# A gated recurrence and a highway layer on one core: two first units of 128 tokens, one shared set of work buffers and a new order

## The chip, the cores and the metric

The kernel runs on one core of a Trainium2 chip. The core has TensorE (PE) for matrix products and transposes, VectorE (DVE), ScalarE (ACT), GpSimd (POOL), and SyncE (SP), which here only starts transfers between the chip's main memory and the core's own memory. Every engine works through its own list of instructions in order and waits where a list says that another engine or a transfer must be done first. The metric is the time of one execution in microseconds (us); several runs are given by their median.

## The reference

```python
def _attn_ref(x, f_logit, lower_bound):              # x: (4, 6336, 256)
    sig = 1.0 / (1.0 + np.exp(-f_logit))
    f = lower_bound + (1.0 - lower_bound) * sig
    i = 1.0 - f
    for t in range(S):
        h = f[:, t] * h + i[:, t] * x[:, t]
        y[:, t] = h

def _moe_ref(x, w_h, w_t, b_t):                      # x: (25344, 256)
    H = np.maximum(x @ w_h, 0.0)
    T = 1.0 / (1.0 + np.exp(-(x @ w_t + b_t)))
    return T * H + (1.0 - T) * x
```

The second function takes the first one's output. Four sequences of 6336 tokens with 256 channels each go through a recurrence along the tokens, and then each token through a highway layer.

## The kernel before, in words

The 25344 tokens, all sequences in a row, are cut into units of 2, 4, 8 or twice 8 blocks of 128 tokens (list `parts`, 21 units numbered from 0). A unit's transfer puts consecutive tokens on each of 128 partitions. Each unit passes through these steps; the letter is the step's name in the order list, and the lines are those of the profile:

- `l` and `x` load f_logit and x (L261, on SP). `u` is the sigmoid of -f_logit (L273, on ACT).
- `i` transposes u on PE, so that channels lie on partitions (L297; two halves of 128 channels). `f` makes 1 - (1 - lower_bound) u from it (L312 on ACT, or L310 on DVE).
- `b` or `B` makes the product u times x (L288, on POOL, or on DVE where the list has a v), one half or the whole of a tile; `p` transposes it on PE, two tokens in one 32-bit word (L322).
- `s` is the recurrence, a scan on DVE from f and the transposed product (L331). Each scan goes on from the last column of the one before, so scans are strictly in order.
- `z` and `g` are the two matrix products of the highway layer on PE (L344, and L149 where the weights in place are used again). `t` is the sigmoid of z (L367, on ACT); `d` joins g and the scan's result on DVE (L374); `e` or `E` multiplies d by t (L388, on POOL, or on DVE with a v).
- `o` brings the result back to tokens on partitions and adds the two parts, with two matmuls for each 128 x 128 piece (L407, L408). `c` copies it out of the accumulators (L427 on ACT, L425 on DVE) and `w` stores it (L434, on SP).
- `k*n` are n dummy matmuls on zeros (L250, L149), which only keep PE busy; six more open the program (L168).

The numbers behind a letter are unit, part or chunk, and half; the number behind the colon is the buffer or the accumulator banks.

No scheduler decides anything: a long string, `order`, lists all steps, and each engine gets its own in the order of that string. SP's loads and stores share one queue in that order, so a store that waits for its copy also holds the loads behind it. Buffers are named in the string too. f_logit and x have five tiles each of 8 KB per partition; u has 4, the product 3, f 4, the scan 6, t 3, d 4 and the output 4 tiles of 4 KB, 28 in all, each kind its own; the last three units' output uses tiles of x. A step that writes a tile waits until the tile's former content has been read.

Parameters come first: `prm` holds lower_bound and b_t, is transposed on PE (`pc`, L212), and DVE makes three small constants of it (`cc`, L216 to L218), which f, d, the scaled weights (`WH`, `WT`) and the diagonal matrix `diag` (`dg`) need.

## Time and profile before

| | |
|---|---|
| Runs | 207.93, 206.80, 207.52 us, median 207.52 us |
| The profiled execution, first to last instruction | 205.8 us |
| Busy: PE, DVE, ACT, POOL | 194.8, 192.4, 190.7, 173.8 us |
| Moved by DMA | 78.67 MB, 382 GB/s over the span |
| Instructions on PE, DVE, ACT, POOL | 1850, 147, 182, 85 |

Busy time is the time in which an engine had an instruction at work, so overlaps count once. For PE it includes the dummy matmuls, and a busy PE is not PE at its peak. The span leaves out what lies before the first and behind the last instruction. In the rows of the profile, `128x1024 bf16<-128x1024 f16` are the shapes and types of result and operand, the first number behind a bar is the sum of busy time, the second the mean in nanoseconds of one instruction, and an arrow names what ended a wait. The clock that PE was granted reads 1.00 in nearly all stretches.

### The profile page before, as it was taken

The numbers are of one execution on the slowest core, as the hardware profiler recorded it, in microseconds if no ns is written. First come the engines' busy times: TensorE is split into PE (matmuls) and PEld (weight loads), VectorE is DVE, ScalarE is ACT, GpSimd is POOL, SyncE is SP. The second block draws the span as 40 slices with busy tenths as digits, with TensorE's granted clock in tenths as the row PEclk, the third lists the DMA queues.
The fourth block names the chain that finished last, engine by engine and source line by source line (L and its number), as shares of the span: only waits on it lengthen the run. The fifth ranks groups of instructions, "written<-read, shape, count | busy, mean of one in ns | idle before, by whom it ended". The sixth has DMA issues, their size and how long they took to land.

```text
span 205.8 us, 4646 instructions
## 1 busy us (share of the span) xinstructions
PE 194.8 (95%) x1850; PEld 135.7 (66%) x1850; DVE 192.4 (93%) x147; ACT 190.7 (93%) x182; POOL 173.8 (84%) x85
## 2 busy tenths in 40 slices
PE   7989999969989999999999999999999999999992
PEld 2555775746765747757757858657757868777671
DVE  0679999999999999999999999999999999999992
ACT  5197999999999999999999999999999999999992
POOL 3634696999999999979999869999899788999760
PEclk9999999999999999999999999999999999999999
DMA  6999999999999999999999999999999999853766
GB/s 191 375 427 419 417 420 419 414 413 426 416 426 427 414 422 410 432 408 427 426 408 426 427 412 425 419 422 427 414 411 407 334 411 382 344 212 140 277 225 234
DMA packets 16700, 78.67 MB, mean 382 GB/s; under 512 B 1828, under 2 KB 2344, under 8 KB 10792
## 3 DMA queue, kind: packets, MB, share of 16 engines
q1 hardware_dynamic: 16672, 78.39, 93.9%
q8 instruction: 14, 0.23, 0.4%
q14 instruction: 6, 0.05, 0.1%
q10 hardware_dynamic: 8, 0.00, 0.0%
HBM read 52.43 MB, written 25.95 MB: 381 GB/s over the span
## 4 chain that ended last, share of the span: by engine, by line
PE 56%; DVE 24%; ACT 7%; issue 5%; DMA 5%; SPq 0%; DVEq 0%; ACTq 0%
PE psum L344 17%; DVE y L331 15%; PE psum L149 13%; DVE d L374 7%; PE psum L407 7%; PE psum L408 7%; PE psum L322 6%; PE psum L297 5%; ACT f L312 4%; DMA x<-in_x_dram 4%; ACT t L367 2%; DMA l<-in_f_logit_dram 1%; ACT u L273 1%; PE psum L250 1%; ACT o L427 1%
## 5 line engine op out<-in xcount | busy, mean ns | idle before, releaser
L288 POOL TENSOR_TENSOR bv<-u,x 128x1024 bf16<-128x1024 f16 (+2 forms) x39 | 101.4, 2615 | 20.0 <-DVE d L388 10.9
L331 DVE TENSOR_TENSOR_SCAN y<-f,y,psum 128x1024 bf16<-128x1024 f16 (+6 forms) x40 | 103.7, 2612 | 0.5 <-PE psum L407 0.4
L344 PE MATMUL psum<-y,w_sb 128*128 128x512 bf16 (+1 forms) x240 | 79.6, 368 | 4.2 <-ACT f L312 1.9
L388 POOL TENSOR_TENSOR d<-d,t 128x1024 bf16<-128x1024 bf16 (+3 forms) x33 | 71.5, 2180 | 4.6 <-ACT o L427 1.3
L374 DVE SCALAR_TENSOR_TENSOR d<-y,ncc,psum 128x1024 bf16<-128x1024 bf16 (+2 forms) x60 | 62.7, 1084 | 1.1 <-PE psum L344 0.4
L149 PE MATMUL psum<-y,w_sb 128*128 128x512 bf16 x168 | 63.6, 379 | 0.0
L367 ACT ACTIVATE t<-psum,bt 128x1024 bf16<-128x1024 f32 (+2 forms) x60 | 57.4, 988 | 0.9 <-PE psum L344 0.5
L273 ACT ACTIVATE u<-l 128x2048 f16<-128x2048 f32 (+2 forms) x28 | 48.1, 1744 | 6.5 <-DMA l<-in_f_logit_dram 6.5
L312 ACT ACTIVATE f<-psum,ncc 128x1024 f16<-128x1024 f16 (+3 forms) x38 | 50.3, 1344 | 1.2 <-PE psum L297 1.2
L407 PE MATMUL psum<-diag,y 128*128 128x128 f16 x396 | 49.7, 219 | 0.2
L408 PE MATMUL psum<-ident_b,d 128*128 128x128 bf16 x396 | 49.7, 219 | 0.0
L408 PEld LDWEIGHTS <-d 128*128 128x128 bf16 x396 | 43.5, 112 | 3.8 <-DVE d L388 0.4
L427 ACT COPY o<-psum 128x1024 f32<-128x1024 f32 (+1 forms) x46 | 44.2, 997 | 1.6 <-ACT f L312 0.6
L407 PEld LDWEIGHTS <-y 128*128 128x128 bf16 x396 | 43.6, 112 | 2.7
L344 PEld LDWEIGHTS <-w_sb 128*128 128x128 f16 x240 | 23.0, 98 | 20.1 <-issue 0.8
L322 PE MATMUL psum<-ident_f,bv 128*128 128x128 f32 x198 | 29.4, 275 | 0.8 <-ACT f L312 0.7
L149 PEld LDWEIGHTS <-w_sb 128*128 128x128 f16 x168 | 16.4, 97 | 20.2 <-issue 5.9
L297 PE MATMUL psum<-ident_h,u 128*128 128x128 f16 x396 | 28.8, 221 | 0.8 <-DVE y L331 0.4
L297 PEld LDWEIGHTS <-u 128*128 128x128 f16 x396 | 25.1, 99 | 5.7 <-issue 1.2
L322 PEld LDWEIGHTS psum<-ident_f,bv 128*128 128x128 f32 x198 | 22.4, 141 | 5.8 <-ACT f L312 1.4
L388 DVE TENSOR_TENSOR d<-d,t 128x1024 bf16<-128x1024 bf16 (+3 forms) x20 | 11.3, 596 | 0.1
L149 PE MATMUL psum<-zeros 128*128 128x512 bf16 x39 | 10.6, 398 | 0.0
(34 smaller groups left out, 43.1 us busy)
## 6 DMA issues: line engine op xcount, KB each, us to landing
l<-in_f_logit_dram SPq DMA_DIRECT2D x23, 1024.0 KB, 13.6
x<-in_x_dram SPq DMA_DIRECT2D x23, 1024.0 KB, 14.2
out_dram<-o SPq DMA_DIRECT2D x43, 512.0 KB, 8.0
out_dram<-x SPq DMA_DIRECT2D x7, 256.0 KB, 2.0
out_dram<-o SPq DMA_DIRECT2D x6, 256.0 KB, 9.3
l<-in_f_logit_dram SPq DMA_DIRECT2D x2, 512.0 KB, 6.5
x<-in_x_dram SPq DMA_DIRECT2D x2, 512.0 KB, 7.3
l<-in_f_logit_dram SPq DMA_DIRECT2D x3, 256.0 KB, 2.8
```

The source lines that it names most:

```text
L149: return pe.add_instruction(mybir.InstMatmult(name=nc.get_next_instruction_name(), start_tensor_calc=start, stop_tensor_calc=stop, tile_si ...
L288: shared(pin(e.tensor_mul(st[n]["bv", s][:, a:c].rearrange("p k d j -> p k j d"), st[n]["u", s][:, 2 * a:2 * c].rearrange("p (k j) d -> p ...
L297: pin(nc.tensor.transpose(uT[:, j * P:(j + 1) * P], st[n]["u", s][:, j, h * P:(h + 1) * P], ident_h))
L312: pin(nc.scalar.activation(to, of, AF.Identity, scale=ncc[:, h:h + 1], bias=1.0))
L322: pin(nc.tensor.transpose(words[:, k:k + g * (P - 1) + 1:g], pair, ident_f))
L331: pin(nc.vector.tensor_tensor_scan(y[:, c:e], st[n]["f", h][:, c:e], data, 0.0 if fresh else carry[h], op0=ALU.mult, op1=ALU.add))
L344: pin(nc.tensor.matmul(p.part(a, e), w, data, start=ki == 0, stop=ki == NH - 1))
L367: pin(nc.scalar.activation(half(n, q, "t", m), z, AF.Sigmoid, bias=bt[:, m:m + 1]))
L374: pin(nc.vector.scalar_tensor_tensor(half(n, q, "d", m), y, ncc[:, m:m + 1], g, op0=ALU.mult, op1=ALU.max))
L388: shared(pin(e.tensor_mul(d, d, t)), not eng)
L407: pin(nc.tensor.matmul(o, st[n]["y", h][:, whole], diag[:, h], start=True, stop=False))
L408: pin(nc.tensor.matmul(o, half(n, q, "d", h)[:, cols], ident_b, start=False, stop=True))
```

## The change

There are 22 units in place of 21: the first two have one block of 128 tokens each, then come one of 2 and one of 4 blocks, and the rest as before with numbers one higher. A product of a unit with one block is made without interleaving two tokens, and transposed as it is.

lower_bound and b_t are loaded into tiles of their own and transposed apart (`pc` and `pb`); b_t is copied by ACT or DVE in a step of its own (`cb`).

All 4 KB tiles (u, product, f, scan, t, d, output) come from one set of 29 (28 before), and the ten 8 KB tiles serve f_logit and x alike. For units of up to 8 blocks f shares one tile for both halves, and so does the scan. The late units no longer take their output tiles from x.

In `products`, the line that picks the engine stands further up; the engine is still DVE where the list has a v, and POOL elsewhere.

The order list is new throughout. It has 23 dummy matmuls behind the first six, where there were 49. More products and gates are made in one piece: POOL has 20 products of a whole tile in place of 12, and 13 gates of 2048 columns in place of 5. DVE has 4 gates of 1024 and 4 of 2048 columns in place of 11 and 1.

Three places of the lists, word for word. Names left of an arrow are written, right of it read; `out_dram` is the output.

First, ACT at the start, before:

```order
L273 ACTIVATE u<-l 128x512 x2
L273 ACTIVATE u<-l 128x1024
L312 ACTIVATE f<-psum,ncc 128x256
L238 ACTIVATE w_sb<-w_raw,cc 128x256 x2
L312 ACTIVATE f<-psum,ncc 128x256
L367 ACTIVATE t<-psum,bt 128x256
L312 ACTIVATE f<-psum,ncc 128x512
L367 ACTIVATE t<-psum,bt 128x256
L273 ACTIVATE u<-l 128x2048
```

and with the change, from the first two sigmoids on:

```order
L289 ACTIVATE u<-l 128x256 x2
L343 ACTIVATE f<-psum,ncc 128x128 x2
L232 COPY bt<-psum 128x2
L289 ACTIVATE u<-l 128x512
L343 ACTIVATE f<-psum,ncc 128x128
L343 ACTIVATE f<-psum,ncc 128x256
L254 ACTIVATE w_sb<-w_raw,cc 128x256 x2
L289 ACTIVATE u<-l 128x1024
L254 ACTIVATE w_sb<-w_raw,cc 128x256 x2
L343 ACTIVATE f<-psum,ncc 128x512
L399 ACTIVATE t<-psum,bt 128x128
L399 ACTIVATE t<-psum,bt 128x256 x2
```

Three more 128-wide t follow, and then the first 2048-wide sigmoid. More and smaller instructions now stand ahead of it.

Second, ACT from the first 2048-wide sigmoid (unit 4) on, with the change:

```order
L289 ACTIVATE u<-l 128x2048
L343 ACTIVATE f<-psum,ncc 128x1024
L455 COPY o<-psum 128x256
L399 ACTIVATE t<-psum,bt 128x512 x2
L289 ACTIVATE u<-l 128x2048
L343 ACTIVATE f<-psum,ncc 128x1024 x2
L455 COPY o<-psum 128x512
L289 ACTIVATE u<-l 128x2048
L343 ACTIVATE f<-psum,ncc 128x1024
L399 ACTIVATE t<-psum,bt 128x1024 x2
L343 ACTIVATE f<-psum,ncc 128x1024
L289 ACTIVATE u<-l 128x2048
```

Here the sigmoids of units 4, 5, 6 and 7 come at closer intervals than those of units 3 to 6 before; behind the row printed last follow f, t, the sigmoid of the first part of unit 8, t, f, a copy of 256 columns, and the sigmoid of the second part.

Third, DVE up to its first 1024-wide scan, before:

```order
L331 SCALAR_TENSOR_TENSOR y<-f,y,psum 128x512 x2
L374 SCALAR_TENSOR_TENSOR d<-y,ncc,psum 128x256 x2
L374 SCALAR_TENSOR_TENSOR d<-y,ncc,psum 128x512
L288 TENSOR_TENSOR bv<-u,x 128x2x2x256
L388 TENSOR_TENSOR d<-d,t 128x256
L374 SCALAR_TENSOR_TENSOR d<-y,ncc,psum 128x512
L388 TENSOR_TENSOR d<-d,t 128x256
L388 TENSOR_TENSOR d<-d,t 128x512
L388 TENSOR_TENSOR d<-d,t 128x256
L331 SCALAR_TENSOR_TENSOR y<-f,y,psum 128x1024 x2
```

and with the change:

```order
L363 SCALAR_TENSOR_TENSOR y<-f,y,psum 128x512 x2
L309 TENSOR_TENSOR bv<-u,x 128x4x2x256
L406 SCALAR_TENSOR_TENSOR d<-y,ncc,psum 128x512 x2
L363 SCALAR_TENSOR_TENSOR y<-f,y,psum 128x1024 x2
L453 COPY o<-psum 128x1024
```

The gates of the first units have left DVE, and the whole product of unit 4 stands there in place of a half of unit 3's. The dummies between unit 3's and unit 5's transposes on PE are the steps `k*9:4`, `k*1:6` and `k*4:7` of the list; on SP, `l19.0:8` takes the 8 KB tile that `x15.0:8` had, and the product that frees it is `B15.0:19`.

The diff; of the order table its first two lines on each side stand for all:

```diff
@@ -39,9 +39,9 @@
     firsts = [b * S for b in range(B)]
 
 
-    CHUNK, GROUP = {17: 4, 18: 4}, {17: 2, 18: 2, 19: 2, 20: 1}
-    JOINED, FROM_X = (20,), (18, 19, 20)
-    parts = [(2,), (2,), (4,), (8,), (8,), (8,), (8,), (8, 8), (8, 8), (8, 8), (8, 8), (8, 8), (8, 8), (8, 8), (8,), (8,), (8,), (8,), (8,), (4,), (2,)]
+    CHUNK, GROUP = {18: 4, 19: 4}, {18: 2, 19: 2, 20: 2, 21: 1}
+    JOINED = (21,)
+    parts = [(1,), (1,), (2,), (4,), (8,), (8,), (8,), (8,), (8, 8), (8, 8), (8, 8), (8, 8), (8, 8), (8, 8), (8, 8), (8,), (8,), (8,), (8,), (8,), (4,), (2,)]
     units, at = [], 0
     for subs in parts:
         units.append((at, subs))
@@ -49,67 +49,67 @@
     assert at == B * S
 
     order = """
-k*4:0 l1.0:0 u1.0:0 i1.0.0:0 i1.0.1:1 l0.0:1 x0.0:0 x1.0:1 u0.0:1 b0.0.0:0 pc:2 wh i0.0.0:3 i0.0.1:4 WI k*1:5 cc
-p0.0.0:2 p0.0.1:5 k*16:6 l2.0:2 u2.0:2 wt b1.0.0:1 p1.0.1:6 f1.0:0 dgv f0.0v:1 f0.1v:2 s0.1:0 x2.0:2 WHv s0.0:1
...
+x0.0:0 l1.0:1 l0.0:2 u0.0:0 x1.0:3 pb:0 pc:1 cc u1.0:1 k*1:6 i0.0.1:7 f0.1:2 b0.0.0:3 i1.0.1:2 l2.0:4 f1.1:4 p0.0.1:3
+i0.0.0:4 f0.0v b1.0.0:5 p0.0.0:5 p1.0.1:6 i1.0.0:1 dg wh WI s0.1:6 cbv s0.0 p1.0.0:7 u2.0:7 i2.0.0:2 i2.0.1:0 s1.1:8
...
@@ -122,6 +122,12 @@
 
     def sb(shape, dtype, name, slot=0):
         return pool.tile(shape, dtype, tag=f"{name}{slot}", name=name)
+
+    def work(dtype, name, slot):
+        return pool.tile([P, 2 * NB * P], dtype, tag=f"work{slot}", name=name)
+
+    def large(name, slot):
+        return pool.tile([P, NB, D], FP32, tag=f"large{slot}", name=name)
 
     psum = ps.tile([P, BANKS * BANK], FP32, tag="psum", name="psum")
 
@@ -167,9 +173,10 @@
     for _ in range(6):
         pin(nc.tensor.matmul(psum[:, 7 * BANK:], zeros[:, :P], zeros, start=True, stop=True))
 
-    prm = sb([2 * NH, P], FP32, "prm")
-    pin(nc.scalar.dma_start(prm[:NH], lower_bound.rearrange("(h p) -> h p", p=P)))
-    pin(nc.scalar.dma_start(prm[NH:], moe_b_t.rearrange("(h p) -> h p", p=P)))
+    raw_lb = sb([NH, P], FP32, "raw_lb")
+    raw_bt = sb([NH, P], FP32, "raw_bt")
+    pin(nc.scalar.dma_start(raw_lb, lower_bound.rearrange("(h p) -> h p", p=P)))
+    pin(nc.scalar.dma_start(raw_bt, moe_b_t.rearrange("(h p) -> h p", p=P)))
     cc = sb([P, NH], FP32, "cc")
     ncc = sb([P, NH], FP32, "ncc")
     bt = sb([P, NH], FP32, "bt")
@@ -208,14 +215,23 @@
         pin((nc.scalar if eng else nc.sync).dma_start(w_raw[:, 0], moe_w_h.rearrange("(h p) o -> p h o", p=P)))
 
     def do_pc(slot, eng):
-        once["prmT"] = Banks(slot).one(0)[:, :2 * NH]
-        pin(nc.tensor.transpose(once["prmT"], prm, ident_f[:2 * NH, :2 * NH]))
+        once["lb"] = Banks(slot).one(0)[:, :NH]
+        pin(nc.tensor.transpose(once["lb"], raw_lb, ident_f[:NH, :NH]))
+
+    def do_pb(slot, eng):
+        once["bt"] = Banks(slot).one(0)[:, :NH]
+        pin(nc.tensor.transpose(once["bt"], raw_bt, ident_f[:NH, :NH]))
 
     def do_cc(slot, eng):
-        prmT = once["prmT"]
-        pin(nc.vector.tensor_scalar(ncc, prmT[:, :NH], 1.0, None, op0=ALU.subtract))
-        pin(nc.vector.tensor_scalar(cc, prmT[:, :NH], -1.0, 1.0, op0=ALU.mult, op1=ALU.add))
-        pin(nc.vector.tensor_copy(bt, prmT[:, NH:]))
+        lb = once["lb"]
+        pin(nc.vector.tensor_scalar(ncc, lb, 1.0, None, op0=ALU.subtract))
+        pin(nc.vector.tensor_scalar(cc, lb, -1.0, 1.0, op0=ALU.mult, op1=ALU.add))
+
+    def do_cb(slot, eng):
+        if eng:
+            pin(nc.scalar.copy(bt, once["bt"]))
+        else:
+            pin(nc.vector.tensor_copy(bt, once["bt"]))
 
     def do_dg(slot, eng):
         for h in range(NH):
@@ -256,7 +272,7 @@
 
     def load(n, s, name, src, slot):
         at, subs = units[n]
-        t = sb([P, NB, D], FP32, name, slot)
+        t = large(name, slot)
         j0 = sum(subs[:s])
         pin(nc.sync.dma_start(t[:, :subs[s]], rows(src, at, j0, j0 + subs[s])))
         st[n][name, s] = t
@@ -269,7 +285,7 @@
 
     def do_u(eng, slot, n, s):
         nb = units[n][1][s]
-        u = sb([P, NB, D], FP16, "u", slot)
+        u = work(FP16, "u", slot).rearrange("p (j d) -> p j d", d=D)
         pin(nc.scalar.activation(u[:, :nb], st[n]["l", s][:, :nb], AF.Sigmoid, scale=-1.0))
         st[n]["u", s] = u
 
@@ -280,11 +296,16 @@
         products(eng, slot, n, s, 0, 2)
 
     def products(eng, slot, n, s, k0, k1):
+        e = nc.vector if eng else nc.gpsimd
         if ("bv", s) not in st[n]:
-            st[n]["bv", s] = sb([P, NB // 2, D, 2], BF16, "bv", slot)
+            st[n]["bv", s] = work(BF16, "bv", slot)
+            if units[n][1][s] > 1:
+                st[n]["bv", s] = st[n]["bv", s].rearrange("p (k d j) -> p k d j", d=D, j=2)
+        if units[n][1][s] == 1:
+            shared(pin(e.tensor_mul(st[n]["bv", s][:, :D], st[n]["u", s][:, 0], st[n]["x", s][:, 0])), not eng)
+            return
         cuts = {2: (0, 1), 4: (0, 1, 2), 8: (0, 2, 4)}[units[n][1][s]]
         a, c = cuts[k0], cuts[k1]
-        e = nc.vector if eng else nc.gpsimd
         shared(pin(e.tensor_mul(st[n]["bv", s][:, a:c].rearrange("p k d j -> p k j d"),
                                 st[n]["u", s][:, 2 * a:2 * c].rearrange("p (k j) d -> p k j d", j=2),
                                 st[n]["x", s][:, 2 * a:2 * c].rearrange("p (k j) d -> p k j d", j=2))), not eng)
@@ -296,10 +317,20 @@
         for j in range(units[n][1][s]):
             pin(nc.tensor.transpose(uT[:, j * P:(j + 1) * P], st[n]["u", s][:, j, h * P:(h + 1) * P], ident_h))
 
+    def halves(n, name, dtype, h, slot):
+
+        N = tokens(n)
+        if N > NB * P:
+            st[n][name, h] = work(dtype, name, slot)[:, :N]
+        elif (name, 0) not in st[n]:
+            both = work(dtype, name, slot)
+            st[n][name, 0], st[n][name, 1] = both[:, :N], both[:, N:2 * N]
+        return st[n][name, h]
+
     def do_f(eng, slot, n, h):
         N, subs = tokens(n), units[n][1]
-        f = sb([P, 2 * NB * P], FP16, "f", slot)
-        to, of = f[:, :N], st[n]["uT", h].all(N)
+        f = halves(n, "f", FP16, h, slot)
+        to, of = f, st[n]["uT", h].all(N)
         if len(subs) == 1:
             to = to.rearrange("c (p j) -> c p j", j=subs[0])
             of = of.rearrange("c (j p) -> c p j", j=subs[0])
@@ -310,11 +341,13 @@
             pin(nc.vector.tensor_scalar(to, of, ncc[:, h:h + 1], 1.0, op0=ALU.mult, op1=ALU.add))
         else:
             pin(nc.scalar.activation(to, of, AF.Identity, scale=ncc[:, h:h + 1], bias=1.0))
-        st[n]["f", h] = f
 
     def do_p(eng, slot, n, s, h):
         if ("bT", h) not in st[n]:
             st[n]["bT", h] = Banks(slot, BF16)
+        if units[n][1][s] == 1:
+            pin(nc.tensor.transpose(st[n]["bT", h].one(s)[:, :P], st[n]["bv", s][:, h * P:(h + 1) * P], ident_b))
+            return
         words = st[n]["bT", h].one(s).bitcast(FP32)
         g = units[n][1][s] // 2
         for k in range(g):
@@ -324,8 +357,7 @@
     carry = {}
 
     def do_s(eng, slot, n, h):
-        y = sb([P, 2 * NB * P], BF16, "y", slot)
-        st[n]["y", h] = y
+        y = halves(n, "y", BF16, h, slot)
         for fresh, c, e in pieces(n):
             data = st[n]["bT", h].part(c, e)
             pin(nc.vector.tensor_tensor_scan(y[:, c:e], st[n]["f", h][:, c:e], data,
@@ -354,7 +386,7 @@
 
     def flat(n, q, name, slot):
         if (name, q) not in st[n]:
-            st[n][name, q] = sb([P, NH * NB * P], BF16, name, slot)
+            st[n][name, q] = work(BF16, name, slot)
         return st[n][name, q]
 
     def half(n, q, name, h):
@@ -414,11 +446,7 @@
         if n in JOINED:
             a, r0 = (j0 - chunk(n, q)[0]) * D, 0
         if ("o", q, r0) not in st[n]:
-            if n in FROM_X:
-                o = sb([P, NB, D], FP32, "x", slot).rearrange("p j d -> p (j d)")
-            else:
-                o = sb([P, 4 * D], FP32, "o", slot)
-            st[n]["o", q, r0] = o
+            st[n]["o", q, r0] = pool.tile([P, 4 * D], FP32, tag=f"work{slot}", name="o")
         op = st[n]["op", q, r].all((j1 - j0) * D)
         to = st[n]["o", q, r0][:, a:a + (j1 - j0) * D]
         if eng:
```

More of the change, by code (lines that the diff above doesn't have):

```diff
@@ new lines @@
+f16.0 E14.1v z15.0.1:01 t15.0.1:1 p16.0.1:2 d15.0.1:28 o14.0.0:34 c14.0.0:9 s16.1:8 p16.0.0:5 s16.0 i18.0.0:7 f18.0
+o14.1.0:01 c14.1.0:23 w8.1.0 l19.0:8 z15.0.0:34 t15.0.0 o13.1.0:67 c13.1.0:16 g15.0.0:01 d15.0.0 u19.0:12 i17.0.1:2
+f17.1:18 g16.0.0:34 d16.0.0:20 g16.0.1:67 d16.0.1 w9.1.0 l20.0:1 o14.0.1:01 B17.0:5 p17.0.1:5 s17.1:25 i17.0.0:3
+c14.0.1:14 p17.0.0:4 f17.0 s17.0 B18.0:2 w11.0.1 z16.0.0:67 t16.0.0:6 z16.0.1:01 t16.0.1 u20.0:3 E15.0 p18.0.1:2
+p18.0.0:3 s18.1:22 o15.0.0:67 c15.0.0:0 o14.1.1:01 c14.1.1:5 o15.0.1:45 c15.0.1:1 g17.0.0:67 d17.0.0:2 w10.1.0 w14.0.0
@@ L113 @@
+d21.0.1:25 o19.0.0:3 c19.0.0:28 w19.0.0 o19.0.1:0 c19.0.1:24 w19.0.1 g21.0.0:5 z21.0.0:2 t21.0.0 e20.0.1v o20.0.0:7
+c20.0.0:7 w20.0.0 o20.0.1:4 c20.0.1:12 w20.0.1 d21.0.0 E21.0v o21.0.1:6 o21.0.0:1 c21.0.0:18 c21.0.1v w21.0.0
 """
```

111 lines of the change are left out of this document (52 added, 59 removed).

## The prediction

> **What bounds the kernel now.** I read the page first, then a table of stretches, then each engine's timeline at the start and the end.
>
> ```profile
> span 205.8 us, 4646 instructions
> PE 194.8 (95%) x1850; PEld 135.7 (66%) x1850; DVE 192.4 (93%) x147; ACT 190.7 (93%) x182; POOL 173.8 (84%) x85
> ```
>
> Three engines are busy for 93% and more, so shares alone name no bound. In the stretches below each pair is busy microseconds and count, in the order of the header:
>
> ```profile
> core 0: us, PE busy (x) PEld busy (x) DVE busy (x) ACT busy (x) POOL busy (x), PEclk, DMA share, GB/s
> 13.85:25.00 11.15, 10.55 (x83) 6.71 (x82) 10.20 (x15) 9.82 (x11) 5.23 (x3) 1.00 1.02 421
> 25.00:202.68 177.68, 171.89 (x1709) 122.58 (x1707) 176.02 (x117) 173.97 (x160) 162.50 (x67) 1.00 0.96 389
> 22.59:202.35 179.76, 174.30 (x1723) 123.85 (x1721) 178.43 (x118) 176.02 (x163) 164.91 (x67) 1.00 0.96 389
> 185.00:190.00 5.00, 5.00 (x54) 3.53 (x52) 5.00 (x5) 5.00 (x8) 5.00 (x4) 1.00 0.34 134
> ```
>
> The two timelines give the edges of these stretches (start, microseconds, instruction):
>
> ```profile
> 22.59 4.58 DVE L331 TENSOR_TENSOR_SCAN y<-f,y,psum 128x1024 bf16<-128x1024 f16 x2 [0.37 <-PE psum L407]
> 201.93 0.42 DVE L425 COPY x<-psum 128x256 f32<-128x256 f32 x1 [0.33 <-PE psum L408]
> ```
>
> ```profile
> 9.35 1.06 ACT L273 ACTIVATE u<-l 128x1024 f16<-128x1024 f32 x1 [4.67 <-DMA l<-in_f_logit_dram]
> 13.85 1.91 ACT L273 ACTIVATE u<-l 128x2048 f16<-128x2048 f32 x1 [0.17 <-DMA l<-in_f_logit_dram]
> 18.90 1.91 ACT L273 ACTIVATE u<-l 128x2048 f16<-128x2048 f32 x1 [0.47 <-DMA l<-in_f_logit_dram]
> 202.31 0.37 ACT L427 COPY x<-psum 128x256 f32<-128x256 f32 x1 [0.52 <-PE psum L408]
> ```
>
> From its first 1024-wide scan at 22.59 DVE works without a gap: 178.43 of 179.76 us, 1.3 lost. DVE sets the pace. ACT is close behind: from its first 2048-wide sigmoid at 13.85 to its last copy at 202.68 it works 9.82 + 173.97 = 183.8 us and loses 1.3 before 25 and 3.7 after. Up to 18.9 both stand on loads: the sigmoids at 9.35, 13.85 and 18.90 start as their data land. The DMA engines are full at 421 GB/s until late and a third busy at 185, so stores do not set the end.
>
> **The change part by part.** *Less in front of the first scan.* Units of one block give data sooner, and DVE's first constants no longer stand behind four dummy matmuls and the first transposes. But every load after them keeps its place in bytes: up to and with unit 4's f_logit the new queue holds 3.67 MB, as the old one did up to unit 3's. So landings past the head can be taken over by bytes. Issue and time to landing of three old loads, the issue rows first:
>
> ```profile
> 0.74 0.85 SPq L261 DMA_DIRECT2D l<-in_f_logit_dram  x2
> 8.03 0.39 SPq L261 DMA_DIRECT2D l<-in_f_logit_dram  x1
> 10.12 0.33 SPq L261 DMA_DIRECT2D l<-in_f_logit_dram  x1
> 13.89 2.82 SPq L261 DMA_DIRECT2D l<-in_f_logit_dram  x2
> ```
>
> ```profile
> l<-in_f_logit_dram SPq DMA_DIRECT2D x1, 1024.0 KB, 16.4
> ```
>
> ```profile
> l<-in_f_logit_dram SPq DMA_DIRECT2D x1, 1024.0 KB, 19.3
> ```
>
> ```profile
> l<-in_f_logit_dram SPq DMA_DIRECT2D x1, 1024.0 KB, 20.5
> ```
>
> These land at 24.4 (7.86 MB, counted from tile sizes), 29.4 (9.96 MB) and 34.4 (12.06 MB). In the new queue those are the places of l6.0, l7.0 and l8.0; l5.0 has the old l4.0's (18.9), and l8.1 ends at 14.16 MB: 2.10 MB at 421 GB/s after 34.4, 39.4.
>
> *ACT's work.* The durations, by shape:
>
> ```profile
> L367 ACT ACTIVATE t<-psum,bt 128x1024 bf16<-128x1024 f32 x42 | 46.7, 1144 | 0.4 <-PE psum L149 0.2
> L273 ACT ACTIVATE u<-l 128x2048 f16<-128x2048 f32 x23 | 44.1, 1947 | 0.7 <-DMA l<-in_f_logit_dram 0.6
> L427 ACT COPY o<-psum 128x1024 f32<-128x1024 f32 x41 | 41.5, 1045 | 1.6 <-ACT f L312 0.6 <-DMA out_dram<-o 0.4 <-PE psum L408 0.2
> L312 ACT ACTIVATE f<-psum,ncc 128x1024 f16<-128x1024 f16 x17 | 19.0, 1139 | 0.8 <-PE psum L297 0.8
> L367 ACT ACTIVATE t<-psum,bt 128x512 bf16<-128x512 f32 x12 | 8.1, 698 | 0.5 <-PE psum L344 0.5
> L367 ACT ACTIVATE t<-psum,bt 128x256 bf16<-128x256 f32 x6 | 2.6, 470 | 0.0
> L427 ACT COPY x<-psum 128x256 f32<-128x256 f32 x1 | 0.4, 373 | 0.5 <-PE psum L408 0.5
> ```
>
> ```profile
> 175.61 1.98 ACT L427 COPY o<-psum 128x1024 f32<-128x1024 f32 x2
> ```
>
> Two copies of 1.045 take 1.98, so I take 0.1 off each instruction for overlap. Behind the first 2048-wide sigmoid the new list has one f of 1024 more (+1.04), two t of 256 fewer (-0.74), two copies of 1024 fewer (-1.89) and two copies of 256 more (+0.54): 183.8 - 1.05 = 182.75 us. All 128-wide pieces stand ahead of it. Their price is in no row: at least 0, at most the 256-wide 0.47; taken 0.27 net each. Behind the 1024-wide sigmoid, which by bytes still starts at 9.35, stand nine or so such small instructions, 3.2 us by this estimate: done at 13.5, so covered by the landing at 13.85. I take 14.2, since some wait for PE; up to 14.5 is free, because unit 5's data come at 18.9 anyway.
>
> From there ACT's own order (second place in the order rows) with net durations: to u5.0 4.4 us, to u6.0 4.4, to u7.0 6.0, to u8.0 3.9, to u8.1 4.2 (the 512-wide copy taken at 0.5, between the 0.37 and 1.05 rows). Starts: u5.0 18.9 (landing), u6.0 24.4 (landing), u7.0 30.4 (work), u8.0 34.4, u8.1 39.4 (landing). Left behind u8.1's start: 182.75 - 22.9 = 159.8 us.
>
> *Two unknowns on ACT.* Four loads of 128 KB take the queue as long to issue as four of 256 KB: two issues more, 0.43 each by the first row, before the same bytes are out. Bounds for all later landings 0 and +0.9; taken +0.5, the middle, since no row is nearer to either end. ACT's later losses: at least 1.3, what the pace-setting engine loses now, at most 3.7, ACT's own now. Taken 2.2, nearer to 1.3 because ACT's role changes. One set of 29 work buffers against 28 of fixed kinds (4+3+4+6+3+4+4) can add or save waits; no row shows those apart, so they lie inside these losses.
>
> *DVE's work.*
>
> ```profile
> L388 DVE TENSOR_TENSOR d<-d,t 128x1024 bf16<-128x1024 bf16 x11 | 7.6, 719 | 0.0
> L425 DVE COPY o<-psum 128x1024 f32<-128x1024 f32 x2 | 2.4, 1208 | 0.3 <-PE psum L408 0.3
> L310 DVE TENSOR_SCALAR f<-psum,ncc 128x1024 f16<-128x1024 f16 x1 | 1.3, 1271 | 0.0
> L288 DVE TENSOR_TENSOR bv<-u,x 128x1024 bf16<-128x1024 f16 x1 | 1.3, 1318 | 0.0
> L388 DVE TENSOR_TENSOR d<-d,t 128x2048 bf16<-128x2048 bf16 x1 | 1.2, 1200 | 0.0
> ```
>
> Behind the first 1024-wide scan, net of 0.07 each: seven fewer gate products of 1024 (-4.5), three more of 2048 (+3.4), two more copies (+2.3), one f fewer (-1.2), small ones -1.05: 178.4 - 1.05 = 177.4. That scan now stands behind a 2048-wide product, twice 1.3 less one fixed part, 2.5 us, which needs x4.0 (4.72 MB, about 16.4 between the rows at 13.85 and 18.90), and two short d: 20.3. With 1.3 lost DVE ends at 199.0, 3.3 earlier than now. So the pace passes from DVE to ACT.
>
> *POOL and the rest.* Halves are joined:
>
> ```profile
> L288 POOL TENSOR_TENSOR bv<-u,x 128x2048 bf16<-128x2048 f16 x12 | 49.5, 4132 | 3.9 <-DVE d L388 3.9
> L288 POOL TENSOR_TENSOR bv<-u,x 128x1024 bf16<-128x1024 f16 x21 | 45.1, 2161 | 9.7 <-DVE d L388 7.0 <-ACT t L367 2.1 <-ACT u L273 0.6
> ```
>
> 4.13 against twice 2.16 saves 0.2 a pair, about what the moved gate products cost; POOL has 32 us free. The line that picks a product's engine only moves up within its function, so "the engines the list means" costs nothing by itself. The two parameter transposes lie ahead of the first data.
>
> *Sum.* ACT ends at 39.4 + 0.5 + 159.8 + 2.2 = 201.9 against 202.7: 0.8 earlier. With the 3.1 us that now follow ACT's last copy the span is 205.0. The profiled execution's 205.8 stands 1.7 below the median of 207.52, so the forecast is 206.7. With the bounds: 39.4 + 159.8 + 1.3 = 200.5 gives 205.3; 39.4 + 0.9 + 159.8 + 3.7 = 203.8 gives 208.6.
>
> **The rivals.** *DVE still sets the end, ACT's landings cost nothing.* If landings come some microseconds sooner, ACT has 14.2 + 182.75 = 197.0 before losses and DVE's 199.0 decides: span 199.0 + 3.5 (now 205.8 - 202.35) = 202.5, time 204.2. For it: ACT's losses now are mostly waits for others. Against: the DMA was already full at 421 GB/s. Chance 0.15.
>
> *A late load waits for a shared buffer.* l19.0 now takes the buffer of x15.0, which POOL frees with unit 15's product. Behind that product POOL has about 43.7 us of work (four products and four gates of 2048 make 33 of it), so with POOL's end near 199 it is done at 155; ACT needs l19.0 32.6 us before its end, at 169. Fourteen microseconds are left:
>
> ```profile
> DMA to landing us min/median/max: 2.7/12.6/20.5
> ```
>
> The median fits, the worst is 6.5 too late. Halfway, 16.6, ACT stands 2.6 us: 209.3. It decides from 14 us on. All that stands behind this sigmoid on ACT waits too. Before, f_logit and x had five buffers each of their own. Chance 0.15.
>
> *Too few dummy matmuls.*
>
> ```profile
> 1.19 2.74 PE L168 MATMUL psum<-zeros 128*128 128x512 bf16 x6 [1.19 <-DVE zeros L166]
> 7.47 3.40 PE L149 MATMUL psum<-zeros 128*128 128x512 bf16 x15
> ```
>
> A 512-wide matmul took 0.46 at first and 0.23 later. The change keeps 23 of 49 dummies after these six. If PE stays at the first rate until 25, the 14 between unit 3's and unit 5's transposes alone cost 14 x 0.23 = 3.2 more, less the 1.1 that ACT waits at u6.0 anyway: 2.1 late, 208.8. It decides when PE is late by more than that wait. Against: PE runs real work for most of that time. Chance 0.10. [...]
>
> **How the numbers follow.** Forecast 0.60, with its own range 205.3 to 208.6; rivals 0.15, 0.15 and 0.10. Changes of under 0.5% (1.04 us) can't be told from none here. The forecast lies at that edge: of its 0.60 I give 0.27 to under 206.5, 0.32 to no change, 0.01 to slower. With the first rival faster is 0.42; with a little of the second, where the load is only just late, no change is 0.34; slower 0.24. The range runs from the first rival to the second, 204.2 to 209.3.
>
> **What would show it.** Right: sigmoids of units 5, 6 and 8 wait for landings near 19, 24 and 39; the first 1024-wide scan near 20; ACT busy about 192 and losing less than now after 40; DVE with 4 us or more idle after 20; the last copy near 202. Wrong: ACT waits that name DVE or PE add up to over 4 us; u19.0 waits for its load; 512-wide matmuls of 0.4 us after 10; landings before 37 for l8.1.

## The result and the profile after

The changed kernel takes **213.56 us** (212.14 to 213.99, 6 runs) against 207.48 us (206.80 to 208.04, 6 runs): ratio **1.0274**, 95% interval 1.0233 to 1.0314, slower by 2.7%. The forecast was 206.7, with a range up to 209.3. It was wrong. Ratios and their intervals, here and below, leave out single executions that ran over 1.5% longer than the fastest of the same kernel, while medians and ranges hold all of them.

The page of the changed kernel: the span, busy time by engine, and in 40 slices the granted clock and the rate of the transfers.

```profile
span 210.2 us, 4570 instructions
PE 192.5 (92%) x1807; PEld 133.1 (63%) x1835; DVE 193.7 (92%) x136; ACT 192.2 (91%) x191; POOL 175.9 (84%) x72
...
PEclk9669999999999999999999999999999999999998
...
GB/s 175 364 423 423 419 418 421 414 416 423 413 424 415 412 421 425 408 423 393 419 423 309 384 337 423 403 376 281 204 384 423 419 414 413 216 363 287 318 285 264
```

ACT's busy time is as forecast (192.2 against about 192); DVE's work is taken up in the table below. The clock falls in slices 2 and 3. From slice 22 on (110 us) the transfers, full until then, drop to 309, 337 and 204 GB/s. In the kernel before they stay above 400 up to slice 31:

```profile
GB/s 191 375 427 419 417 420 419 414 413 426 416 426 427 414 422 410 432 408 427 426 408 426 427 412 425 419 422 427 414 411 407 334 411 382 344 212 140 277 225 234
```

The windows that answer to the forecast's sums are ACT from u8.1 to its last copy, and DVE from its first 1024-wide scan to its last copy:

```profile
core 0: us, PE busy (x) PEld busy (x) DVE busy (x) ACT busy (x) POOL busy (x), PEclk, DMA share, GB/s
22.19:206.58 184.39, 174.10 (x1703) 123.10 (x1726) 180.44 (x113) 177.26 (x164) 165.91 (x50) 1.00 0.95 380
41.27:206.73 165.46, 158.65 (x1569) 113.25 (x1593) 161.53 (x101) 160.00 (x149) 147.87 (x43) 1.00 0.95 376
```

The edges of these windows, from the two timelines:

```profile
13.85 0.69 ACT L343 ACTIVATE f<-psum,ncc 128x512 f16<-128x512 f16 x1 [2.54 <-PE psum L318]
...
16.33 1.93 ACT L289 ACTIVATE u<-l 128x2048 f16<-128x2048 f32 x1
...
41.27 1.96 ACT L289 ACTIVATE u<-l 128x2048 f16<-128x2048 f32 x1
...
206.36 0.37 ACT L455 COPY o<-psum 128x256 f32<-128x256 f32 x1 [0.19 <-issue]
```

```profile
22.19 2.34 DVE L363 TENSOR_TENSOR_SCAN y<-f,y,psum 128x1024 bf16<-128x1024 f16 x1
...
206.16 0.42 DVE L453 COPY o<-psum 128x256 f32<-128x256 f32 x1 [0.51 <-PE psum L440]
```

| | forecast | measured | difference |
|---|---|---|---|
| first 2048-wide sigmoid, u4.0 | 14.2 | 16.33 | +2.1 |
| first 1024-wide scan | 20.3 | 22.19 | +1.9 |
| u8.1 starts (39.4 + 0.5) | 39.9 | 41.27 | +1.4 |
| ACT's work behind it | 159.8 | 160.0 | +0.2 |
| ACT's idle time behind it | 2.2 | 5.46 | +3.3 |
| ACT's last copy ends | 201.9 | 206.73 | +4.8 |
| DVE's work behind that scan | 177.4 | 180.44 | +3.0 |
| DVE's idle time behind it | 1.3 | 3.95 | +2.7 |
| DVE's last copy ends | 199.0 | 206.58 | +7.6 |

So there are two places: the start, and what both engines lose later. The later loss lies around 128 to 167 us. POOL's timeline, then DVE's and ACT's at the same time:

```profile
134.76 4.11 POOL L309 TENSOR_TENSOR bv<-u,x 128x2048 bf16<-128x2048 f16 x1 [2.45 <-DMA out_dram<-o]
...
151.51 4.12 POOL L309 TENSOR_TENSOR bv<-u,x 128x2048 bf16<-128x2048 f16 x1 [2.49 <-DMA out_dram<-o]
...
159.61 4.14 POOL L309 TENSOR_TENSOR bv<-u,x 128x2048 bf16<-128x2048 f16 x1
166.20 8.21 POOL L309 TENSOR_TENSOR bv<-u,x 128x2048 bf16<-128x2048 f16 x2 [2.44 <-DVE d L420]
```

```profile
161.32 4.65 DVE L420 TENSOR_TENSOR d<-d,t 128x2048 bf16<-128x2048 bf16 x2
```

```profile
127.95 1.01 ACT L455 COPY o<-psum 128x1024 f32<-128x1024 f32 x1 [1.03 <-DMA out_dram<-o]
...
147.18 2.02 ACT L455 COPY o<-psum 128x1024 f32<-128x1024 f32 x2
...
155.12 1.91 ACT L289 ACTIVATE u<-l 128x2048 f16<-128x2048 f32 x1 [1.19 <-DMA l<-in_f_logit_dram]
```

Two products, B14.0 and B15.0, wait for *stores*: each takes a work buffer in which a finished output still lies. The first of two gates on DVE, E14.0, starts at 161.32 while POOL is inside the product at 159.61. The two gates take 4.65 us; one took 1.20 in the kernel before. ACT waits for a store at 127.95 and for the load l17.0 at 155.12. SP's timeline shows why one of these stores and the load are late; all 117 of its issues stand in the order of the list:

```profile
121.33 9.22 SPq L462 DMA_DIRECT2D out_dram<-o  x3
...
145.39 3.27 SPq L462 DMA_DIRECT2D out_dram<-o  x2
148.75 0.42 SPq L277 DMA_DIRECT2D l<-in_f_logit_dram  x1
```

The group at 121.33 is w5.0.1, w9.1.1, w11.0.0. Tile 9.1.1 had been copied out by 97.82, and its store was issued only at 122.58; B14.0 needs its buffer. Then SP stands until copy c11.0.0 is done at 130.20, with everything else behind it, and again until c12.0.1 at 145.37. l17.0 stands in the list behind w12.0.1 and w12.1.0, so it is issued at 148.75 and lands at 155.10.

B15.0's buffer is another case. Its tile 12.1.0 is the first of the two copies at 147.18, done at 148.29, and its store is issued at 148.32, at once. But the list gives this buffer to the very next product, so B15.0 waits for the landing although the store was not put off. ACT's copies at 127.95 and 129.19, too, wait for stores that were issued within 0.03 us of their copies and took 9.4 and 8.7 us to land. So the shared buffers cost in two ways: a store comes late, or a buffer's next user comes too soon.

Over all stores, matched by the list to their copies in the timelines, the issue follows the end of the copy by 13.8 us on average and 69.5 at most, where the kernel before had 1.1 and 15.1. Counting each tile until 3 us behind its issue (chosen for the count; the median store of 512 KB took 9.7 us to land, 8.0 before), up to 11 finished tiles lie in work buffers at once; before, the four output buffers held at most 4.

### The profile page after: what moved, and what is told of

Its sections match the earlier page's. It is cut to its first block, busy times and chain, and to the rows that moved or that the text cites. A ratio compares the mean times of both kernels' runs of the same rounds, so it can differ in the third digit from the quotient of the medians.

```text
span 210.2 us, 4570 instructions
## 1 busy us (share of the span) xinstructions
PE 192.5 (92%) x1807; PEld 133.1 (63%) x1835; DVE 193.7 (92%) x136; ACT 192.2 (91%) x191; POOL 175.9 (84%) x72
## 4 chain that ended last, share of the span: by engine, by line
PE 55%; ACT 25%; issue 7%; DMA 6%; DVE 4%; SPq 1%; ACTq 0%; DVEq 0%
PE psum L376 17%; PE psum L155 10%; PE psum L439 8%; ACT t L399 8%; PE psum L440 7%; PE psum L355 7%; ACT u L289 6%; ACT f L343 6%; PE psum L318 5%; ACT o L455 5%; DMA out_dram<-o 4%; DMA x<-in_x_dram 2%; DVE y L363 1%; DVE d L406 1%; SPq L277 1%
## 5 line engine op out<-in xcount | busy, mean ns | idle before, releaser
L309 POOL TENSOR_TENSOR bv<-u,x 128x2048 bf16<-128x2048 f16 (+2 forms) x27 | 96.5, 3587 | 17.1 <-DVE d L420 6.9
L363 DVE TENSOR_TENSOR_SCAN y<-f,y,psum 128x1024 bf16<-128x1024 f16 (+7 forms) x42 | 104.4, 2511 | 1.7 <-PE psum L355 1.4
L376 PE MATMUL psum<-y,w_sb 128*128 128x512 bf16 (+2 forms) x244 | 79.1, 364 | 5.6 <-DVE y L363 2.3
L420 POOL TENSOR_TENSOR d<-d,t 128x2048 bf16<-128x2048 bf16 (+4 forms) x28 | 76.2, 2732 | 7.7 <-DVE d L406 5.5
L406 DVE SCALAR_TENSOR_TENSOR d<-y,ncc,psum 128x1024 bf16<-128x1024 bf16 (+3 forms) x62 | 62.7, 1057 | 3.2 <-PE psum L376 2.0
L399 ACT ACTIVATE t<-psum,bt 128x1024 bf16<-128x1024 f32 (+3 forms) x62 | 58.0, 963 | 2.6 <-PE psum L155 1.6
L343 ACT ACTIVATE f<-psum,ncc 128x1024 f16<-128x1024 f16 (+4 forms) x41 | 52.3, 1293 | 4.1 <-PE psum L318 3.7
L289 ACT ACTIVATE u<-l 128x2048 f16<-128x2048 f32 (+3 forms) x29 | 48.5, 1697 | 4.2 <-DMA l<-in_f_logit_dram 4.2
L455 ACT COPY o<-psum 128x1024 f32<-128x1024 f32 (+2 forms) x52 | 46.5, 922 | 2.7 <-DMA out_dram<-o 1.3
L420 DVE TENSOR_TENSOR d<-d,t 128x1024 bf16<-128x1024 bf16 (+2 forms) x10 | 10.6, 1076 | 0.4 <-ACT t L399 0.4
```

What stands on the lines that cost most here:

```text
L309: shared(pin(e.tensor_mul(st[n]["bv", s][:, a:c].rearrange("p k d j -> p k j d"), st[n]["u", s][:, 2 * a:2 * c].rearrange("p (k j) d -> p ...
L343: pin(nc.scalar.activation(to, of, AF.Identity, scale=ncc[:, h:h + 1], bias=1.0))
L363: pin(nc.vector.tensor_tensor_scan(y[:, c:e], st[n]["f", h][:, c:e], data, 0.0 if fresh else carry[h], op0=ALU.mult, op1=ALU.add))
L376: pin(nc.tensor.matmul(p.part(a, e), w, data, start=ki == 0, stop=ki == NH - 1))
L399: pin(nc.scalar.activation(half(n, q, "t", m), z, AF.Sigmoid, bias=bt[:, m:m + 1]))
L406: pin(nc.vector.scalar_tensor_tensor(half(n, q, "d", m), y, ncc[:, m:m + 1], g, op0=ALU.mult, op1=ALU.max))
```

## The experiments

Two theories. **Start**: too few dummy matmuls leave PE at half rate (the third rival; the clock reads 0.50 from 8 to 14 us), all is 1.4 to 2 us late, and this reaches the end. **Buffers and stores**: the next user of a shared buffer comes before the store of the finished output in it has landed, products come late, and a late product meets a gate. The rival to both: the new order of the engines' own work costs the time. Ratios are to the kernel before, run alongside.

**Nine and four more dummies**, ahead of p2.0.1 and p3.0.0:

```diff
-x2.0:5 f1.0 b2.0.0v:9 p2.0.1:4
+x2.0:5 f1.0 b2.0.0v:9 k*9:3 p2.0.1:4
...
-d0.0.1 p3.0.0:3
+d0.0.1 k*4:3 p3.0.0:3
```

> The changed kernel with 13 more dummy matmuls: nine ahead of the first transposed product of unit 2 and four ahead of that of unit 3. Theory 'cold start': the matrix engine stood 1.7 us before 8.39 us and then ran at half rate (granted clock 0.50 from 8 to 14 us), which delayed everything behind it by about 2 us. Expected by it: clock 1.00 from 8 to 14 us, the first 2048-wide sigmoid at 14.4 to 14.8 us instead of 16.33, the one of l8.1 at 39.4 to 40 instead of 41.27, and the time 1.3 to 2.0 us lower (about 0.7 to 0.9 %). Rival 'the middle decides': the stores and buffers of 120 to 160 us set the end whatever the start does, and the time stays within 0.5 us. A third: the dummies delay the transposes themselves, and the first wide sigmoid stays at 16 us or later.

213.25 us, ratio 1.0277 (1.0215 to 1.0340): no change. Nine dummies in a row still ran at the slow rate (0.63 us for the one at 6.56, then 3.35 for eight; five at 10.84 took 1.24) and held p2.0.1 until 10.17. The first wide sigmoid came at 15.35, between the two expectations, and u8.1 at 40.84, 0.4 earlier. So the dummies went elsewhere:

```diff
+k*1:6  (ahead of p0.0.1:3)
+k*1:2  (ahead of p1.0.1:6)
+k*1:4  (ahead of i2.0.0:2)
+k*6:3  (ahead of p2.0.1:4)
```

> The changed kernel with nine more dummy matmuls, laid between the first transposes (one each ahead of p0.0.1, p1.0.1 and i2.0.0, six ahead of p2.0.1) instead of thirteen in front of two of them as in the run warm, where nine of them ran at the slow rate and themselves held the transposes back to 10.17 us. Theory 'start': the matrix engine is at full rate from about 6 us, the first 1024-wide scan starts near 20.7 instead of 22.19 us and the sigmoid of l8.1 near 39.9 instead of 41.27. The run warm showed 0.4 us of start and 0.3 us in the time; if a start that is 1.3 us earlier reaches the end, the time falls by 1.3 us; rival 'the stores decide': the copy c11.0.1, which waits for a store that lands at 128 us whatever the start does, then waits 2.5 us instead of 1.03, and the time falls by less than 0.5 us.

The start does what was forecast for it. ACT's and DVE's timelines of this run:

```profile
14.28 1.95 ACT L290 ACTIVATE u<-l 128x2048 f16<-128x2048 f32 x1
```

```profile
40.35 1.91 ACT L290 ACTIVATE u<-l 128x2048 f16<-128x2048 f32 x1 [0.48 <-DMA l<-in_f_logit_dram]
```

```profile
20.46 4.60 DVE L364 TENSOR_TENSOR_SCAN y<-f,y,psum 128x1024 bf16<-128x1024 f16 x2
```

14.28, 20.46 and 40.35, now waiting for its landing: the forecast had 14.2, 20.3 and 39.9. The time is 212.70 us, ratio 1.0256 (1.0226 to 1.0285), overlapping the changed kernel's: the start's 0.9 to 2 us do not reach the end. They are given back here:

```profile
156.55 1.91 ACT L290 ACTIVATE u<-l 128x2048 f16<-128x2048 f32 x1 [3.10 <-DMA l<-in_f_logit_dram]
```

In the changed kernel this wait for l17.0 was 1.19. The copy c11.0.1 waits 1.45 for its store instead of 1.03.

**The kernel before with fewer dummies** (2 for 16 in the longest run of them, `k*16:6` to `k*2:6`):

> The kernel before with 2 instead of 16 dummy matmuls in its longest run of them (7.3 to 10.7 us). It prices the granted clock alone. Theory 'cold start': the matrix engine stands about 3 us there, the granted clock falls to 0.50 for some microseconds behind it, and the first 1024-wide scan moves by 0.5 to 2 us; as the first wide sigmoids wait for landings (18.9 us) the time rises by 0 to 1 us. Rival: no loss of clock, and the time stays within 0.3 us or falls, because transposes no longer queue behind dummies.

207.88 us, ratio 1.0006 (0.9978 to 1.0034). No loss of clock either:

```profile
7.00:11.00 4.00, 1.18 (x8) 0.57 (x7) 2.96 (x6) 1.80 (x4) 1.99 (x3) 1.00 1.03 388
11.00:14.00 3.00, 2.75 (x24) 1.77 (x22) 2.74 (x6) 2.62 (x7) 1.57 (x2) 1.00 1.03 434
```

PE works 1.18 of 4 us and keeps the full rate behind it: three 512-wide matmuls at 12.89 take 0.81 us, as do the three at 13.06 in the kernel before. The 14 dummies taken out here carry no price.

**B15.0 in a buffer of its own** (one work buffer more; the raw weights take the place of a later tile):

```diff
-    w_raw = sb([P, 2, NH, D], FP32, "w_raw")
+    w_raw = pool.tile([P, 2, NH, D], FP32, tag="work28", name="w_raw")
...
-d14.1.0 B15.0:19 p15.0.0:0
+d14.1.0 B15.0:29 p15.0.0:0
```

> The changed kernel with one more work buffer, used by one product alone, B15.0 (the raw weights share a buffer with a later tile to make room). In the changed kernel this product waits 2.49 us for a store, and the DVE gate E14.0 then stands 2.4 us behind the next product. Theory 'late stores hold shared buffers': the wait at 151.5 us goes, products B15.0, B16.0 start some 2.4 us earlier, the gate E14.0 takes about 1.2 us instead of 3.5, and the time falls by 1 to 2.4 us. Rival 'another wait takes its place': the wait goes and the gate is short, but VectorE then waits as long for projections of unit 15, because the late load l17.0 holds ScalarE for 1.2 us at 155; the time falls by 0.5 us at most.

212.57 us, 1.0207 (1.0137 to 1.0276). The wait goes and so does the long gate. POOL's, DVE's and ACT's timelines:

```profile
149.38 4.16 POOL L309 TENSOR_TENSOR bv<-u,x 128x2048 bf16<-128x2048 f16 x1
```

```profile
161.54 2.34 DVE L420 TENSOR_TENSOR d<-d,t 128x2048 bf16<-128x2048 bf16 x2
164.71 1.28 DVE L406 SCALAR_TENSOR_TENSOR d<-y,ncc,psum 128x1024 bf16<-128x1024 bf16 x1 [0.83 <-ACT o L455]
```

```profile
155.70 1.91 ACT L289 ACTIVATE u<-l 128x2048 f16<-128x2048 f32 x1 [1.32 <-DMA l<-in_f_logit_dram]
```

Both gates take 2.34 us instead of 4.65. B14.0 still waits 2.43 us for its store. DVE now waits, first for ACT, 2.0 us between 160 and 180 in all, and ACT still waits for l17.0. Most of the gain turns into a new wait.

**Load l17.0 ahead of the two stores, alone:**

```diff
-l18.0:1 c12.0.1:22 ... w12.0.1 ... w12.1.0 l17.0:7
+l18.0:1 l17.0:7 c12.0.1:22 ... w12.0.1 ... w12.1.0
```

> The changed kernel with load l17.0 ahead of the stores of 12.0.1 and 12.1.0 on SP, and nothing else: the half of own_l17 that own leaves out. In the changed kernel ScalarE waits 1.19 us for this load at 155 us. If the two waits are two losses in a row the time falls by about as much as from own to own_l17 (0.9 %, 1.9 us). If they lie side by side (the product B15.0 still waits for the store w12.1.0, which is now issued behind one more load and lands later, and VectorE's scan and its gate wait for the products anyway), the wait for the load goes and the time stays within 0.5 %: only both together help.

213.53 us, 1.0321 (1.0281 to 1.0361): no gain. ACT finds its load, B15.0 still waits 2.76 us, and the pair of gates is as long as ever. POOL, then DVE:

```profile
152.47 4.12 POOL L309 TENSOR_TENSOR bv<-u,x 128x2048 bf16<-128x2048 f16 x1 [2.76 <-ACT o L455]
```

The row names ACT's copy, but that had ended at 148.52; B15.0 starts 0.16 us behind the landing of the store w12.1.0 at 152.31.

```profile
162.28 4.65 DVE L420 TENSOR_TENSOR d<-d,t 128x2048 bf16<-128x2048 bf16 x2
```

**Both together:**

> As the run own, and load l17.0 issued before the stores of 12.0.1 and 12.1.0 instead of behind them, so that it does not stand 10 us behind SP's wait for a copy. Theory 'late stores' with the load as its second half: the wait of ScalarE for l17.0 (1.19 us at 155) goes too, VectorE finds its projections, and the time falls by 2 to 3 us against the changed kernel. Rival 'the order is short of work in its last third': both waits go, and the time still falls by less than 1 us, since the waits come back as waits for the matrix engine after 180 us.

210.72 us, **1.0116** (1.0055 to 1.0178). ACT and DVE:

```profile
153.38 3.86 ACT L289 ACTIVATE u<-l 128x2048 f16<-128x2048 f32 x2
```

```profile
162.58 2.33 DVE L420 TENSOR_TENSOR d<-d,t 128x2048 bf16<-128x2048 bf16 x2
```

Neither sigmoid at 153 waits, and DVE's idle time between 160 and 180 falls to 0.55. One half gives 0.5 to 0.7% at most, the other nothing, both together 1.6%. The losses lie side by side on two engines that are equally full.

The changed kernel and the run `own` were run once more beside `l17`:

> The changed kernel itself once more, beside the two halves: about 1.027 of the kernel before. Its profile also tells how far one wait moves from execution to execution: the wait of B15.0 for its store and the gate E14.0 (2.49 and 3.51 us) are expected again within 0.5 us, the start within 0.5 us.

> The run own again, next to the changed kernel itself and l17, since own's interval (1.014 to 1.028) holds both no gain and a gain of 1.3 %. Own waits for a load (1.3 us) and for projections (2.0 us on VectorE after 160 us) took the place of the 2.3 us that the gate no longer lost; expected is a gain of 0 to 1 us, less than 0.5 %.

The changed kernel gave 213.44 us, 1.0284 (1.0253 to 1.0315); own 212.07 us, 1.0235 (1.0206 to 1.0264). Both ratios lie within the intervals of the first runs. Within this one comparison the private buffer is worth 0.5%, and the two intervals touch (1.0253 to 1.0315, 1.0206 to 1.0264): about half a per cent, and no more certain than that. The changed kernel's second profile comes from an execution of 216.38 us. In it B15.0 waits 2.81 us, near the 2.49, but the two gates take 2.92 us and the first wide sigmoid starts at 17.78, so two of the three expectations were missed. own's profile repeats:

```profile
162.62 2.34 DVE L420 TENSOR_TENSOR d<-d,t 128x2048 bf16<-128x2048 bf16 x2
165.64 1.28 DVE L406 SCALAR_TENSOR_TENSOR d<-y,ncc,psum 128x1024 bf16<-128x1024 bf16 x1 [0.68 <-ACT o L455]
```

The two gates take 2.34 us again, and DVE again waits for ACT behind them.

**Both, with the dummies of warm2:**

> The run own_l17 with the dummies of warm2: B15.0 in a buffer of its own, load l17.0 ahead of two stores, nine more dummy matmuls at the start. The runs so far: own_l17 is 1.2 % above the kernel before, warm2 alone changes the changed kernel's time by less than 0.5 %. If the two are separate losses the time falls a further 0.6 to 1.3 us, to within 0.6 % of the kernel before; if the copy c11.0.1, which waits for the store w10.0.1, takes the start's gain whole (it waited 1.03 us in the changed kernel, 2.54 in own_l17, and the store lands at 127 to 129 us whatever the start does), it stays at 1.2 %.

210.10 us, 1.0118 (1.0082 to 1.0155): no difference to own_l17 that could be measured. The copy c11.0.1 waits 1.66 us for the store w10.0.1. That is less than the 2.54 in own_l17, so this copy does not take the start's gain here; what takes it is open.

**Same engine work, other stores and buffers.** TensorE, VectorE, ScalarE and GpSimd keep their order row for row, `mem` that of the changed kernel, `mem_warm` and `rob` that of warm2. SP's order and the buffers' numbers are new, with 30 buffers. `mem` and `mem_warm` were laid out without a margin for slow transfers, `rob` with one. SP's list around the place, the changed kernel and `rob`:

```diff
-x13.1 x15.0 w10.0.0 l16.0 l15.0 x14.1 x21.0 w10.0.1 w11.1.0 x14.0 w5.0.1 w9.1.1 w11.0.0 x18.0 x16.0 w10.1.1 x20.0 l18.0 w12.0.1 w12.1.0 l17.0
+x13.1 w9.1.1 x13.0 w8.1.1 x14.1 w8.0.0 w9.1.0 l14.0 w6.0.0 l14.1 w10.0.0 x15.0 w10.0.1 l15.0 x14.0 l16.0 w11.0.0 w9.0.0 w8.1.0 w11.0.1 w10.1.1 l17.0
```

> The changed kernel with the same instructions in the same order on TensorE, VectorE, ScalarE and GpSimd, row for row; different are only the order of loads and stores on SP, the numbers of the buffers, and one more work buffer (30; the raw weights share one). Theory 'buffers and stores': with no buffer held by a late store, the waits of the middle go (POOL for stores 4.9 us, ScalarE for stores and for l17.0 2.5 us, the gate E14.0 of 3.5 us), the last copy ends 2 to 3 us earlier, and the time is 2 to 3.5 us below the changed kernel's, near 210 to 211.5. Rival 'the order of the engines itself': it falls by less than 1 us.

> The run mem with the dummies of warm2. If start and middle add, the time falls by the sum of both (3.5 to 4.5 us below the changed kernel, 209 to 210); if nothing of the middle holds any more, the earlier start reaches the end in full (1.3 us below mem); rival: it stays within 0.5 us of mem. By the sum of both it would still not be below the kernel before (207.5): 1 to 2 us would be left, which then lie in the order of the engines' work.

> The engines' instructions in the order of warm2 row for row; loads and stores in another order on SP, buffers numbered anew with one more of them, chosen so that a product, copy or scan still finds its buffer free when transfers run 3 % slower (the run mem was chosen without that margin and lost 2.0 us at 178 us to one store). Theory 'buffers and stores': waits for stores and loads after 60 us fall under 0.5 us on every engine and the time is 1 to 1.5 % below the changed kernel, 0.8 to 1.5 % above the kernel before or less. Rival 'the order of the engines itself costs the rest': it stays 1 % or more above the kernel before although no engine waits for a transfer; what then stands between them is waits of GpSimd for VectorE's gates and the start.

mem 212.71 us, 1.0219 (1.0178 to 1.0260); mem_warm 212.05 us, 1.0178 (1.0130 to 1.0226); rob **209.74 us, 1.0137** (1.0106 to 1.0168). mem was expected at 210 to 211.5 us and mem_warm at 209 to 210, and both missed: without a margin the waits come back elsewhere, as in mem_warm's ACT timeline.

```profile
176.34 2.12 ACT L400 ACTIVATE t<-psum,bt 128x1024 bf16<-128x1024 f32 x2 [0.83 <-DMA out_dram<-o]
```

In rob, behind 60 us, ACT waits 0.25 us for one load and DVE for no transfer. POOL still waits up to 1.2 us for one, so there the 0.5 of the expectation was missed. At most 7 finished tiles lie in buffers. A store is still issued 7.6 us behind its copy on average, against 1.1 in the kernel before; what went are nearly all the waits of a buffer's next user. The two windows of the forecast:

```profile
20.76:203.78 183.02, 173.89 (x1730) 123.25 (x1727) 179.05 (x113) 176.79 (x164) 166.62 (x50) 1.00 0.98 387
40.83:203.95 163.12, 158.31 (x1594) 113.31 (x1593) 159.62 (x102) 159.78 (x149) 148.60 (x43) 1.00 0.97 383
```

ACT: 40.83 + 159.78 + 3.34 idle = 203.95. The idle time is back within the forecast's bounds (1.3 to 3.7), and the last copy is 2.8 us earlier than in the changed kernel. It is still 1.3 later than in the kernel before. DVE's work falls from 180.44 to 179.05, but its idle time stays: 183.02 - 179.05 = 3.97. None of the versions beats the kernel before.

Against warm2 (1.0256), whose engine lists it shares, rob gains 1.2%. Its 1.4% above the kernel before lies in both ranges that were written down for it (0.8 to 1.5%, and 1% or more for the rival), so rob does not decide between them.

What stays open: about half of the loss, 1.2% in own_l17 and 1.4% in rob. Against the forecast's 201.9 rob's last copy is 2.05 us late. Of this 0.9 is a start still later than forecast (40.83 against 39.9; ACT stands 2.78 us for DVE at 25.5, because of a buffer of rob's own numbering). The other 1.1 is ACT's idle time, 3.34 against 2.2, in short waits, about half of them in the last 25 us. No run took these away, and none tested the new order of the engines' work apart, so that rival is not ruled out for this half.

## Why the prediction was wrong

**The step that failed** is "One set of 29 work buffers against 28 of fixed kinds can add or save waits; no row shows those apart, so they lie inside these losses." The losses were taken at 2.2 for ACT (bounds 1.3 to 3.7) and 1.3 for DVE; ACT lost 5.46, and DVE 3.95 idle and 2.3 more inside a gate. Both bounds came from a kernel in which outputs have buffers of their own and a store follows its copy by 1.1 us on average. The new list hands a buffer with a finished output to a product, a copy or a scan, and the price came out there: 2.45 us at B14.0, 2.49 at B15.0, then the gate behind it. A load behind waiting stores on SP's list, l17.0, added 1.19 on ACT. The runs show this share: own_l17, with the load moved as well, gives back 1.6% of the 2.7%, and rob 1.2% against warm2. In rob ACT's idle time is 3.34 and the gate is short, while DVE's idle time is still 3.97. So DVE's 1.3 was too small for a further reason, and the cause of that stays open.

**Point by point.**

- *DVE's work, 177.4*: 180.44. The gate E14.0 accounts for 2.3 (3.51 us in the changed kernel, 1.20 in own); the other 0.7 was not taken apart. The forecast priced a 2048-wide gate at 1.2 from its one row, and said nothing of where POOL would be.
- *The pace passes to ACT*: no. ACT and DVE end 0.15 us apart, and own and l17 show that freeing one of them gives next to nothing.
- *ACT's work, 159.8*: 160.0. *Landings by bytes*: right as far as they show. warm2's u8.1 waits for its landing and starts at 40.35 (39.9 forecast, just past the bound of 40.3); in the changed kernel the sigmoids of units 5 to 8 came too late to wait at all.
- *The start, 14.2 and 20.3*: 16.33 and 22.19, because PE was slow. x2.0 lands at 7.45, its product goes to p2.0.1 at 8.39, and PE, which had stood 1.73 us, works at half rate until about 14 (the clock reads 0.50 from 8 to 14; the five dummies below take 2.34 us, seven at 16.51 take 1.67):

```profile
8.39 0.47 PE L355 MATMUL psum<-ident_f,bv 128*128 128x128 f32 x1 [1.73 <-DVE bv L309]
...
9.77 2.34 PE L155 MATMUL psum<-zeros 128*128 128x512 bf16 x5
```

- *The third rival* had the kind of loss right, but not its place. It priced 14 dummies between unit 3's and unit 5's transposes at the slow rate until 25; these ran at the fast one (seven 512-wide matmuls at 16.51 in 1.67 us). The loss came from dummies and matmuls between 8.4 and 14 us. That its size came near (1.4 to 2.1 against 2.1) is luck. It is wrong in its price at the end: warm2 removed the late start and the time did not follow. The forecast took a late start to add to the end in full; in warm2 the waits for l17.0 and at c11.0.1 grew by 2.3 us together, more than the 0.9 gained at u8.1.
- *The second rival* (a late load behind a shared buffer): the right kind, the wrong tile. u19.0 did not wait. l17.0 did, because SP stood at two stores ahead of it, and the buffers that cost were the work buffers, not the large ones.
- *The first rival* (DVE ends at 199.0): no.
- *What would show it*: two of the four signs of "wrong" came: ACT's waits for PE came to 7.1 us in all, and 512-wide matmuls of 0.4 us after 10.
- From ACT's +4.8 to the median: the tail behind ACT's last copy is 3.5 instead of 3.1 (+0.4), the profiled execution's 212.21 stands 2.0 above its span where 1.7 was added (+0.3), and the median is 1.35 above that execution. 4.8 + 0.4 + 0.3 + 1.35 = 6.85, the whole of 213.56 - 206.7.

## What to carry to other kernels

A shared pool of buffers turns the order of stores, and the choice of each buffer's next user, into a schedule for the compute engines: follow each buffer from its store's place on the issuing queue, through the store's landing, to the next tile that takes it. Here two engines were equally full, and removing one engine's wait showed next to nothing; remove the waits of both before judging either. Bounds for waits that were read from one allocation do not bound another.
